# A rebuilt first stage, and g of tiles 4 to 7 moved, in a fused attention-and-MLP kernel scheduled by a list scheduler

## Chip, cores, metric

One core of one Trainium2 chip. The metric is the device time of one execution in microseconds. "Ratio" is always the mean time of one kernel's fast runs over the mean of the fast runs of the kernel before in the same rounds on the same chip, so it is not quite the ratio of the medians quoted beside it. The interval given with it is 95%.

## The reference

x is 2048 tokens by 448, bf16. After a layer norm it goes through linear attention with 16 heads of 28 (s) and through a squared-ReLU MLP of 1792 (whose silu is g). The output is x + s * g.

```python
def reference(A_x, A_wqkv, A_wo, B_x, B_w1, B_b1, B_w2, B_b2):
    # _A_ref: q, k, v = x @ wqkv; phi(t) = where(t > 0, t + 1, exp(t)) + 1e-6
    #   kv = sum_s phi(k) v, z = sum_s phi(k), o = phi(q) kv / (phi(q) z + 1e-6), o @ wo
    # _B_ref: relu(x @ w1 + b1)**2 @ w2 + b2
    x = A_x
    xn = _layernorm(x, axis=-1)
    s = _A_ref(xn, A_wqkv, A_wo)
    g = _silu(_B_ref(xn, B_w1, B_b1, B_w2, B_b2))
    return x + s * g
```

## The kernel before

The tokens are 16 tiles of 128, in four groups of four tiles. For each group the kernel computes K of each tile (phi of k), Q (three chunks), and H0 to H13 (the MLP's hidden layer, transposed). Then come the sums over tokens, the denominators, g of each tile, and S of each tile (attention output, multiplied by g). x is normalized, and must be transposed (xT) before any of these matmuls. The contraction is 448 = 3 x 128 + 64, so two units share the last 64 rows: their half-row matmuls run side by side on the two halves of TensorE ("pairs").

The program is a list of operations with modelled durations. A list scheduler decides, before anything runs, the order on each engine. TensorE and SyncE (SP) keep the order of the text; ACT, DVE and POOL take the ready operation that the model thinks is needed soonest. On the chip each engine then works through its fixed list and waits where it must.

```python
RATE = 262e3                    # modelled bytes per us of all loads together
LEAD = 8.0
# ... cut (in schedule): modelled transfers
                s2 = max(dma_free, st + 1.9)
                dma_free = s2 + op.nbytes / RATE
                op.end = dma_free + 0.7
# ... cut: loads, in issue order
        load_x(0, 1, "act")
        load_x(1, 2)                                   # on SP
        load_k("sp", w_qkv, A_wqkv, "wk", 384, 2 * D)  # K weights
        load_x(2, 4, "act")
        dma("act", b1r[:, :], B_b1.rearrange("(f p) -> f p", p=P), ["b1r"], F * 2).prio = -103
        load_w1("w1a", 0, 512)                         # h weights of H0 to H3
        load_x(4, 8)
        # ... cut: further weights; then the ACT table load, prio -101

        def pe_transpose(si, eng, prio):               # one tile: five transposes, one copy
            b = Buf("T")
            def f(e, _):
                v = ps(b)[:, :].bitcast(bf)
                for c in range(3):
                    e.transpose(v[:, c * P : (c + 1) * P], xn[:, si, c * P : (c + 1) * P], ident[:, :])
                e.transpose(v[0:64, 3 * P : 4 * P], xn[:, si, 384:448], ident[:, :])
                return e.transpose(v[64:P, 3 * P : 4 * P], xn[:, si, 384:448], ident[:, :])
            # ... cut: copy of the bank to xT on ACT or DVE

        def dma_transpose(si):                         # tiles 4 to 15 are transposed by a transfer
            op = add("sp", ...)                        # ... cut
            op.lead = LEAD + STAGGER * (3 - si % 4)    # how early it should be issued
# ... cut: the head
        warm(10, wide=True)                            # matmuls on zeros, to have the clock up
        pe_transpose(0, "act", -100)
        warm(2)
        pe_transpose(1, "dve", at_head["xT1"])
        pe_two(kk(0), kk(1), third_and_fourth)         # K0, K1; tiles 2 and 3 transposed between
        streams = (("H0 H1 H2 H3 K2 H4 K3 H6", "H5 Q0 Q1 H7 H8 H9 Q2 H11 H10 K0' H12 H13"), ...)
# ... cut: denominators. Their reciprocals go to DRAM and come back broadcast over partitions (rb);
#     DVE then multiplies q by them, group by group
        def replicate(eng, dst, src, h, step, n, name, reads):   # one broadcast; 19 in all
            # ... cut
            dma(eng, dst.rearrange("p (g t) -> p g t", g=NG), src, [name], dst.shape[0] * NG * n * 2, reads)
# ... cut: the last stage; (first g tile, first S tile of each pair)
        for i, *pairs in ((4, 0), (6, 2), (8, 4, 6), (10, 8), (12, 10, 12)):
```

Of the kernel before, what the change touches and what calls it, by code (L numbers as in the profile page):

```python
# [9 lines left out]
P = 128  # L10
# [7 lines left out]
RATE = 262e3  # L18
# [14 lines left out]
class Op:  # L33
    def __init__(self, eng, emit, reads, writes, dur, alts, nbytes):
        self.eng, self.emit, self.dur, self.alts, self.nbytes = eng, emit, dur, alts, nbytes
        self.reads, self.writes = list(reads), list(writes)
        self.raw, self.deps, self.succ = set(), set(), []
        self.start = self.end = None
        self.seq = None
        self.late = 1e9  # L40
        self.lead = LEAD
        self.prio = None
        self.sync = set()
# [10 lines left out]
class Program:  # L54
# [3 lines left out]
    ENGINES = ("pe", "act", "dve", "pool", "sp")  # L58
# [27 lines left out]
    def schedule(self):  # L86
# [25 lines left out]
        free["pool"] = free["dve"] = 0.8  # L112
# [7 lines left out]
        def ready(op):  # L120
            r = 0.0
            for d in op.deps:
                if d.end is None:
                    return None
                r = max(r, d.end + (0.0 if d.eng == op.eng == "pe" and d not in op.sync else LAT))
            return r
# [14 lines left out]
        while n:  # L141
# [69 lines left out]
            if op.nbytes:  # L211
                free[e] = st + op.dur
                s2 = max(dma_free, st + 1.9)
                dma_free = s2 + op.nbytes / RATE
                op.end = dma_free + 0.7
# [65 lines left out]
def bass_recurrent_scan__linear_attn_block__dense_activation_squared_relu__prompt_kernel(  # L281
    nc, A_x, A_wqkv, A_wo, B_x, B_w1, B_b1, B_w2, B_b2, out
):
    with ExitStack() as es:
# [5 lines left out]
        junk = sb("junk", [P, 512], bf)  # L290
# [14 lines left out]
        b1r = sb("b1r", [NF, P], bf)  # L305
# [33 lines left out]
        def pool(fn, writes, reads=(), dur=0.3):  # L339
            add("pool", fn, reads, writes, dur)  # L340
# [4 lines left out]
        add("dve", lambda e, _: e.memset(junk[:, :], 0.0), [], ["junk"], 0.2).prio = -1000  # L345
# [29 lines left out]
        pool(lambda e, _: e.memset(zmask[:, :, :], 1.0), ["zmask"])  # L375
# [19 lines left out]
        def load_x(lo, hi, eng="sp"):  # L395
            dma(eng, x_tok[:, lo:hi, :], x_r[:, lo:hi, :], [("x", i) for i in range(lo, hi)], (hi - lo) * P * D * 2)

        def load_k(eng, w, src, name, lo, hi, eng2=None):

            n = (hi - lo) * 2  # L400
            dma(
                eng, w[:, 0:3, lo:hi], src[0:384, lo:hi].rearrange("(c p) j -> p c j", p=P), [(name, 0)], 384 * n
            )
            for i in (0, 1):
                dma(eng2 or eng, w[64 * i : 64 * i + 64, 3, lo:hi], src[384:448, lo:hi], [(name, 1 + i)], 64 * n)

        def load_w1(name, lo, hi):


            dma(  # L410
                "sp", w_1[:, 0:3, lo:hi], B_w1[0:384, lo:hi].rearrange("(c p) j -> p c j", p=P), [(name, 0)],
                768 * (hi - lo),
            )
# [5 lines left out]
        wnames = lambda name: [(name, i) for i in range(3)]  # L419
        load_x(0, 1, "act")  # L420
        load_x(1, 2)
        load_k("sp", w_qkv, A_wqkv, "wk", 384, 2 * D)
        load_x(2, 4, "act")
        dma("act", b1r[:, :], B_b1.rearrange("(f p) -> f p", p=P), ["b1r"], F * 2).prio = -103
        load_w1("w1a", 0, 512)
# [4 lines left out]
        add("act", lambda e, _: e.preload_act_table_set("natural_log_exp_and_others"), [], ["actw"], 1.3).prio = -101  # L430

# [10 lines left out]
        def ln_stats(si, prio=(None, None)):  # L442
            add(
                "dve", lambda e, _: e.bn_stats(st6[:, si, :], x_tok[:, si, :]), [("x", si)], [("st", si)], 0.553  # L444
            ).prio = prio[0]
            add(
                "dve", lambda e, _: e.bn_aggr(mv[:, si, :], st6[:, si, :]), [("st", si)], [("mv", si)], 0.16
            ).prio = prio[1]

        def ln_rstd(lo, hi):  # L450
            c = slice(lo, hi)
            ts = range(lo, hi)
            add(
                "act",
                lambda e, _: e.activation(out=vep[:, c], in_=mv[:, c, 1], func=AF.Ln, bias=eps5[:, 0:1]),
                [("mv", i) for i in ts] + ["eps5", "actw"], [("vep", i) for i in ts], 0.2,
            )
            add(
                "act", lambda e, _: e.activation(out=rstd[:, c], in_=vep[:, c], func=AF.Exp, scale=-0.5),
                [("vep", i) for i in ts], [("rstd", i) for i in ts], 0.2,  # L460
            )

        def ln_norm(si, prio=None):
            add(
                "dve",
                lambda e, _: e.tensor_scalar(  # L466
                    out=xn[:, si, 0:D], in0=x_tok[:, si, :], scalar1=mv[:, si, 0:1],
                    scalar2=rstd[:, si : si + 1], op0=ALU.subtract, op1=ALU.mult,
                ),
                [("x", si), ("mv", si), ("rstd", si)], [("xn", si)], 0.43,  # L470
            ).prio = prio

        def ln_twin(lo, hi):

            ts = range(lo, hi)
            add(
                "dve", lambda e, _: e.tensor_copy(xn[:, lo:hi, 448:512], xn[:, lo:hi, 384:448]), [("xn", i) for i in ts],
                [("xd", i) for i in ts], 0.1 + 0.03 * (hi - lo),
            )

        def pe_transpose(si, eng, prio):
            b = Buf("T")

            def f(e, _):
                v = ps(b)[:, :].bitcast(bf)
                for c in range(3):
                    e.transpose(v[:, c * P : (c + 1) * P], xn[:, si, c * P : (c + 1) * P], ident[:, :])  # L487
                e.transpose(v[0:64, 3 * P : 4 * P], xn[:, si, 384:448], ident[:, :])  # L488
                return e.transpose(v[64:P, 3 * P : 4 * P], xn[:, si, 384:448], ident[:, :])

            add("pe", f, [("xn", si), "ident"], [b], 0.35)

            def ev(e, _):
                src = ps(b)[:, 0:256].bitcast(bf).rearrange("p (c k) -> p c k", c=4)
                dst = xT[:, :, si * P : (si + 1) * P]
# [4 lines left out]
            add(eng, ev, [b], [("xT", si)], 0.42 if eng == "dve" else 0.6).prio = prio  # L500

        def dma_transpose(si):
# [5 lines left out]
            op.lead = LEAD + STAGGER * (3 - si % 4)  # L508
# [43 lines left out]
        def pe_two(a, b, between):  # L552

            for u in (a, b):

                def f(e, _, u=u):
                    for k in range(3):
                        last = u.mm(e, 2, k, k == 0, False)
                    return last

                add("pe", f, u.reads, [u.bank], 3 * MM(u.n))
            between()

            def rest(e, _):
                a.mm(e, 0, 3, False, True)
                return b.mm(e, 1, 3, False, True)

            add("pe", rest, [r for u in (a, b) for r in [*u.reads, u.bank]], [a.bank, b.bank], MM(a.n) + 0.1)
            a.out()
            b.out()  # L570
# [20 lines left out]
        def kk(si):  # L591
# [10 lines left out]
            return Acc(b, [("xT", si)] + wnames("wk"), mm, lambda: phi(b, qk_of(si), ("pk", si), blocks), 512)  # L602
# [21 lines left out]
        def qq(g, m):  # L624
# [8 lines left out]
            reads = [("xT", 4 * g + i) for i in range(4)] + wnames("wq")  # L633
            return Acc(b, reads, mm, lambda: phi(b, pqT[:, m, g * 512 : (g + 1) * 512], ("pq", g, m), lambda a: a), 512)

        def hh(g, fi):
            b = Buf("H")

            def mm(e, h, c, start, stop):
                return e.matmul(  # L640
                    ps(b)[:, 0:512], w_1[half[h], c, fi * P : (fi + 1) * P], xT[half[h], c, g * 512 : (g + 1) * 512],
# [3 lines left out]
            def out():  # L645
# [9 lines left out]
                def sq(e, eng):  # L655
                    if eng == "dve":
# [5 lines left out]
            return Acc(b, [("xT", 4 * g + i) for i in range(4)] + wnames(w1_of(fi)), mm, out, 512)  # L662
# [333 lines left out]
        order = ["st0", "mv0", "st1", "mv1", "xn0", "st2", "xn1", "mv2", "st3", "mv3", "xT1", "xn2", "xn3", "xT2", "xT3"]  # L996
        at_head = {n: -100 + i for i, n in enumerate(order)}
        for si in range(4):
            ln_stats(si, (at_head[f"st{si}"], at_head[f"mv{si}"]))
            ln_rstd(si, si + 1)  # L1000
            ln_norm(si, at_head[f"xn{si}"])

        def warm(n, after=(), wide=False):
            b = Buf("W")

            def f(e, _):
                last = None
                for _i in range(n):
                    w = 512 if wide else P
# [3 lines left out]
            add("pe", f, ["junk", *after], [b], n * (0.426 if wide else 0.107))  # L1013
            return b

        warm(10, wide=True)
        pe_transpose(0, "act", -100)
        warm(2)
        pe_transpose(1, "dve", at_head["xT1"])

        def third_and_fourth():
            pe_transpose(2, "act", -100)
            pe_transpose(3, "dve", at_head["xT3"])

        pe_two(kk(0), kk(1), third_and_fourth)
        bb = Buf("B1")
        add(
            "pe", lambda e, _: e.transpose(ps(bb)[:, 0 : NF // 2].bitcast(bf), b1r[:, :], ident[0:NF, 0:NF]),
            ["b1r", "ident"], [bb], 0.1,
        )  # L1030
        add(
            "act", lambda e, _: e.activation(out=b1f[:, :], in_=ps(bb)[:, 0 : NF // 2].bitcast(bf), func=AF.Copy), [bb],
            ["b1f"], 0.25,
        )

        def quads(g, what):
# [11 lines left out]
            ("H0 H1 H2 H3 K2 H4 K3 H6", "H5 Q0 Q1 H7 H8 H9 Q2 H11 H10 K0' H12 H13"),  # L1048
# [4 lines left out]
        for g, (first, second) in enumerate(streams):  # L1053
            if g + 1 < NG:
                ln(4 * g + 4, 4 * g + 8)
            quads(g, first)
# [36 lines left out]
        for i, *pairs in ((4, 0), (6, 2), (8, 4, 6), (10, 8), (12, 10, 12)):  # L1093
            ga, gb = gg(i), gg(i + 1)
            us = [(ss(j), ss(j + 1)) for j in pairs]
            phase((ga, C), (gb, C))
            x, y = us[0]
            if len(us) == 1:
# [49 lines left out]
```

## Time and profile before

Median 143.47 us (three runs, 143.30 to 143.54). The profiled execution spans 142.0 us.

| what | us | where read |
|---|---|---|
| TensorE busy | 137.8 of 142.0 | busy table |
| copy of transposed tile 3 (xT3) ends | 9.56 | timeline |
| H0 to H3 | 9.62 to 12.65 | timeline |
| quad K2 H4 K3 H6 begins | 12.65 | matmul start times |
| from there to the last matmul start | 126.52 | matmul start times |

The busy table of the page (engine, busy us, share of the span, instructions):

```profile
PE 137.8 (97%) x1215; PEld 67.4 (47%) x1215; DVE 91.3 (64%) x218; ACT 78.7 (55%) x151; POOL 23.4 (17%) x37
```

The waits of TensorE (who waited for whom: total us, times, longest):

```profile
PE pb L1010 <- DVE junk L345: 1.3, 1, 1.3
PE pb L487 <- DVE xn L466: 0.2, 1, 0.2
```

Line 1010 is the warm-up and line 487 a transpose: both are over before 5.6 us. After that no wait is listed. A busy share alone does not say that TensorE works at its pace, so I also took each matmul's start from the trace and compared the step to the next one with columns / 2.4 ns. From 12.65 us to the end the steps that are visibly longer add up to 0.8 us, none by more than 0.11 us. So this part cannot be shortened by removing waits, and the head is where time can come from.

The chain of waits in the head (start us, us, what; followed back from the last instruction):

```profile
0.80 2.78 DMA x_tok<-in_A_x_dram
3.61 0.64 DVE st L444
...
6.35 0.34 PE pb L487 x3
...
6.87 1.43 PE pb L597 x6
...
9.14 0.44 DVE xT L497
...
9.62 3.19 PE pb L640 x28
12.81 0.86 PE pb L597 x8
```

It alternates between engines: load, stats on DVE (444), transposes (487), K0 and K1 (597), the copy of tile 3 on DVE (497), H0 to H3 (640), then the quad with K2. **H0 to H3 need all four tiles, so they wait for the last copy.** That copy in turn waits for TensorE, which has the transposes of tiles 2 and 3 behind K0 and K1: DVE ended the norm of tile 3 at 8.11 and then stood 1.0 us idle (last line below). Here is what DVE does from the first load to that copy (groups by shape; busy us, mean ns | idle us before):

```profile
L444 DVE BATCH_NORM_STATS2 st<-x_tok 128x6 f32<-128x448 bf16 x5 | 3.1, 610 | 2.4 <-DMA x_tok<-in_A_x_dram 2.4
L466 DVE TENSOR_SCALAR xn<-x_tok,mv,rstd 128x448 bf16<-128x448 bf16 x4 | 1.5, 382 | 0.0
L497 DVE COPY xT<-pb 128x512 bf16<-128x512 bf16 x2 | 0.8, 408 | 1.0 <-PE pb L489 1.0
```

Later in the run, around the first S, the timeline shows (start us, us, engine, line, operation, shapes, [idle before]): the add of g 3 (916), the casts of msb (776), and the multiplication of q by the broadcast reciprocals (866). S (971) follows without a wait.

```profile
95.22 0.62 DVE L916 TENSOR_TENSOR gbuf<-pb,b2b 128x448 bf16<-128x448 f32 x1 [1.76 <-PE pb L905]
...
95.98 1.19 DVE L776 CAST msb<-pb 128x448 bf16<-128x448 f32 x2
...
97.32 0.96 DVE L866 TENSOR_TENSOR pqT<-pqT,xT 128x1536 bf16<-128x1536 bf16 x1
...
99.11 0.35 PE L971 MATMUL pb<-msb,pqR 64*128 64x448 bf16 x2
```

### The profile page before, as it was taken

The page shows a single profiled execution, that of the slowest core. Times are in us where ns is not written, and L with a number is a line of the kernel's source. Part 1 is how long each engine was busy: PE and PEld are TensorE (multiplying, and loading weights), DVE is VectorE, ACT ScalarE, POOL GpSimd, SP SyncE. Part 2 cuts the span into 40 slices and gives each one's busy share as a digit, 9 for nine tenths or more (in the row PEclk, how much of TensorE's full clock was granted, in tenths as well). Part 3 has the DMA queues.
Part 4 walks back from the last instruction along what each step waited for, and adds up shares of the span by engine and source line. Part 5 has one row for each costly group of instructions (what it writes and reads, how often), then busy time and mean ns, then how long its engine had stood idle before and what let it go on. Part 6 is the DMA issues. An engine that isn't in the chain of part 4 may idle for free.

```text
span 142.0 us, 3024 instructions
## 1 busy us (share of the span) xinstructions
PE 137.8 (97%) x1215; PEld 67.4 (47%) x1215; DVE 91.3 (64%) x218; ACT 78.7 (55%) x151; POOL 23.4 (17%) x37
## 2 busy tenths in 40 slices
PE   6999999999999999999999999999999999999992
PEld 2344444444444444444445455654555555555482
DVE  0979698698897999678959900149852436052743
ACT  2667979889878898879799572323030211030220
POOL 6000000000000000000790000000050507350670
DMA  4997768999250300000000025891001110201022
GB/s 111 329 334 225 78 176 279 342 244 129 55 64 15 74 19 5 0 9 14 0 0 0 0 78 135 186 166 32 5 6 58 37 32 32 97 27 43 32 97 67
DMA packets 19809, 12.90 MB, mean 91 GB/s; under 512 B 9364, under 2 KB 19412, under 8 KB 19796
## 3 DMA queue, kind: packets, MB, share of 16 engines
q1 hardware_dynamic: 17644, 11.22, 32.5%
q10 hardware_dynamic: 2152, 1.50, 4.8%
q8 instruction: 9, 0.15, 0.4%
q14 instruction: 4, 0.03, 0.1%
HBM read 8.78 MB, written 2.10 MB: 77 GB/s over the span
## 4 chain that ended last, share of the span: by engine, by line
PE 93%; DVE 3%; DMA 2%; issue 0%; DVEq 0%
PE pb L905 30%; PE pb L640 30%; PE pb L597 8%; PE pb L971 8%; PE pb L672 6%; PE pb L628 6%; DMA x_tok<-in_A_x_dram 2%; DVE st L444 1%; PE pb L678 1%; PE pb L765 1%; PE pb L726 1%; PE pb L487 1%; PE pb L803 0%; DVE xn L466 0%; PE pb L488 0%; DVE xT L497 0%
## 5 line engine op out<-in xcount | busy, mean ns | idle before, releaser
L640 PE MATMUL pb<-xT,w 64*128 64x512 bf16 x392 | 50.8, 376 | 0.1
L905 PE MATMUL pb<-w,r 64*128 64x448 bf16 (+3 forms) x378 | 45.1, 343 | 0.0
L649 ACT ACTIVATE r<-pb,b1f 128x512 bf16<-128x512 f32 x56 | 34.9, 689 | 4.1 <-PE pb L640 4.1
L640 PEld LDWEIGHTS pb<-xT,w 64*128 64x128 bf16 x392 | 21.4, 94 | 23.3 <-ACT r L649 0.6
L905 PEld LDWEIGHTS pb<-w,r 64*128 64x128 bf16 (+1 forms) x378 | 22.9, 95 | 19.9 <-issue 1.2
L916 DVE TENSOR_TENSOR gbuf<-pb,b2b 128x448 bf16<-128x448 f32 (+1 forms) x16 | 9.3, 609 | 33.2 <-PE pb L905 33.2
L881 ACT ACTIVATE gbuf<-gbuf 128x448 bf16<-128x448 bf16 (+1 forms) x16 | 8.6, 565 | 36.2 <-DVE gbuf L916 34.4
L950 POOL TENSOR_TENSOR xn<-xn,x_tok 128x448 bf16<-128x448 bf16 x15 | 15.1, 1029 | 48.7 <-DVE xn L941 48.7
L597 PE MATMUL pb<-w_qkv,xT 64*128 64x512 bf16 (+1 forms) x106 | 17.6, 377 | 0.0
L628 PE MATMUL pb<-xT,w_qkv 64*128 64x512 bf16 x84 | 15.5, 376 | 0.0
L657 DVE TENSOR_TENSOR r<-r 128x512 bf16<-128x512 bf16 x38 | 13.2, 418 | 0.0
L382 POOL MEMSET kvm<- 128x2048 bf16 x1 | 1.8, 1804 | 65.0 <-DVE zb L622 65.0
L971 PE MATMUL pb<-msb,pqT 64*128 64x448 bf16 (+3 forms) x93 | 11.2, 343 | 0.0
L444 DVE BATCH_NORM_STATS2 st<-x_tok 128x6 f32<-128x448 bf16 x16 | 9.4, 612 | 2.4 <-DMA x_tok<-in_A_x_dram 2.4
L575 ACT ACTIVATE qk<-pb 128x512 bf16<-128x512 f32 x16 | 9.0, 594 | 3.3 <-PE pb L597 2.7
L585 DVE SCALAR_TENSOR_TENSOR qk<-pb,qk 128x512 bf16<-128x512 f32 x16 | 10.7, 686 | 0.2
L941 DVE TENSOR_TENSOR xn<-pb,gbuf 128x448 bf16<-128x448 f32 (+2 forms) x17 | 9.3, 590 | 1.9 <-ACT gbuf L881 1.5
L658 ACT ACTIVATE r<-r 128x512 bf16<-128x512 bf16 x18 | 10.4, 651 | 0.0
L597 PEld LDWEIGHTS pb<-w_qkv,xT 64*128 64x128 bf16 (+1 forms) x106 | 6.6, 94 | 6.5 <-DVE xT L497 0.3
L672 PE MATMUL pb<-qk,xn 128*128 128x448 bf16 x48 | 9.4, 353 | 0.0
L628 PEld LDWEIGHTS pb<-xT,w_qkv 64*128 64x128 bf16 x84 | 6.0, 94 | 5.0
L616 DVE TENSOR_TENSOR zacc<-zacc,qk 128x448 f32<-128x448 f32 x13 | 8.1, 622 | 0.3
(81 smaller groups left out, 98.6 us busy)
## 6 DMA issues: line engine op xcount, KB each, us to landing
out_dram<-xn SPq DMA_DIRECT2D x15, 112.0 KB, 1.7
w<-in_B_w_dram SPq DMA_DIRECT2D x1, 1568.0 KB, 9.7
x_tok<-in_A_x_dram SPq DMA_DIRECT2D x3, 448.0 KB, 4.4
w<-in_B_w_dram SPq DMA_DIRECT2D x2, 384.0 KB, 4.7
xT<-rows ACTq DMA_DIRECT2D x6, 112.0 KB
w<-in_B_w_dram SPq DMA_DIRECT2D x1, 576.0 KB, 5.3
xT<-rows SPq DMA_DIRECT2D x5, 112.0 KB
w_o<-in_A_wo_dram SPq DMA_DIRECT2D x1, 392.0 KB, 10.9
```

Source lines behind the costliest of these rows:

```text
L444: "dve", lambda e, _: e.bn_stats(st6[:, si, :], x_tok[:, si, :]), [("x", si)], [("st", si)], 0.553
L585: lambda e, _: e.scalar_tensor_tensor(out=slot, in0=src(), scalar=1.0 + 1e-6, in1=slot, op0=ALU.add, op1=ALU.max),
L597: return e.matmul(ps(b)[:, 0:512], xT[half[h], c, si * P : (si + 1) * P], w_qkv[half[h], c, 384 : 2 * D], start=start, stop=stop,)
L628: return e.matmul(ps(b)[:, 0:512], w_qkv[half[h], c, m * P : (m + 1) * P], xT[half[h], c, g * 512 : (g + 1) * 512], start=start, stop=stop,)
L640: return e.matmul(ps(b)[:, 0:512], w_1[half[h], c, fi * P : (fi + 1) * P], xT[half[h], c, g * 512 : (g + 1) * 512], start=start, stop=stop,)
L649: lambda e, _: e.activation(out=slot, in_=ps(b)[:, 0:512], func=AF.Relu, bias=b1f[:, fi : fi + 1]),
L657: return e.tensor_tensor(out=slot, in0=slot, in1=slot, op=ALU.mult)
L658: return e.activation(out=slot, in_=slot, func=AF.Square)
L672: last = e.matmul(ps(b)[:, 0:D], xn[:, si, c * P : (c + 1) * P], pk_of(si), start=(si == 0), stop=(si == NT - 1),)
L905: return e.matmul(ps(b)[:, 0:n], r2[half[h], fi, si * P : (si + 1) * P], w_2[half[h], fi, c], start=start, stop=stop)
L950: eng, lambda e, _: e.tensor_tensor(out=ob, in0=ob, in1=x_tok[:, si, c], op=ALU.add),
L971: return e.matmul(ps(b)[:, 0:n], q, m, start=start, stop=stop)
```

## The change

The intent is to have useful matmuls begin earlier and fill TensorE's gaps in the head. It has these parts:

1. x tile 0 on SP and tile 1 on ACT; the ACT table load ahead of ACT's issues; h weights of H0 to H3 in two parts.
2. Norm, transposes and copies of tiles 0 and 1 in column halves; only 128x128 transposes (the last 64 columns are copied beside themselves by DVE, so no half-row transposes).
3. H0 to H3 begin on the 256 tokens of tiles 0 and 1, and get the other 256 after tiles 2 and 3.
4. New modelled transfer times, a fixed order of DVE and ACT in the head, and less urgency for the transposes of tiles 4 to 7.
5. In the last stage, g 4 to 7 ahead of the first S.
6. Not in the cuts below: the warm-up matmuls read a constant instead of a tile that DVE must first fill, so they begin at 0.84 us instead of 1.26. No run takes this part back alone.

```diff
-RATE = 262e3
+RATE = 300e3
 ...
-                s2 = max(dma_free, st + 1.9)
+                s2 = max(dma_free, st + 1.75)
                 dma_free = s2 + op.nbytes / RATE
-                op.end = dma_free + 0.7
+                op.end = dma_free + 0.3
 ...
-        load_x(0, 1, "act")
-        load_x(1, 2)
+        table = add("act", lambda e, _: e.preload_act_table_set("natural_log_exp_and_others"), [], ["actw"], 0.1)
+        table.prio = -120
+        load_x(0, 1)
+        load_x(1, 2, "act").prio = -118
 ...
-        load_w1("w1a", 0, 512)
+        load_w1("w1a", 0, 512, 2)
 ...
-            op.lead = LEAD + STAGGER * (3 - si % 4)
+            op.lead = LEAD + STAGGER * (3 - si % 4) if si > 7 else 4.0 + 1.4 * (7 - si)
 ...
+        k0, k1 = kk(0), kk(1)
+        first = [hh(0, fi, 0) for fi in range(4)]
+        second = [hh(0, fi, 1, first[fi].bank) for fi in range(4)]
 ...
+        turn(0, 0, "act")
+        turn(0, 1, "act")
+        turn(1, 0, "act")
+        mains(k0, (0, 1), [("xT", 0, 0)] + wnames("wk")[:1])
+        turn(1, 1, "dve")
+        mains(k0, (2,), [("xT", 0, 1)])
+        k_mains(k1, 1)
 ...
+        h_mains(0)
+        h_mains(1)
+        head["xT2"] = pe_transpose(2, None, "act")
+        h_mains(2)
+        head["xT3"] = pe_transpose(3, None, "dve")
+        h_mains(3)
 ...
+        rests(k0, k1)
 ...
+        rests(first[0], first[2])
+        rests(first[1], first[3])
+        for eng, names in (
+            ("dve", "st0 mv0 st1 mv1 xn00 xn01 xd0 xn10 xn11 xd1 st2 mv2 xT11 st3 mv3 xn2 xd2 xn3 xd3 xT3"),
+            ("act", "ln0 ex0 ln1 ex1 xT00 xT01 xT10 ln2 ex2 b1 ln3 ex3 xT2"),
+        ):                                   # ... cut: each becomes the fixed order of its engine
+        pe_four(*second)
 ...
-        for i, *pairs in ((4, 0), (6, 2), (8, 4, 6), (10, 8), (12, 10, 12)):
+        phase((g4, C), (g5, C))
+        phase((g6, C), (g7, C))
+        phase((g5, C), (g4, C))
+        s0[0]()
+        phase((g7, C), (g6, C))
+        s0[1]()
+        for i, *pairs in ((8, 2, 4), (10, 6, 8), (12, 10, 12)):
```

## The prediction

> **What bounds it now.** TensorE: the busy table gives it 97% of a 142.0 us span. The timeline's matmul starts show more: from the K2/H4 quad, at 12.65 us, to the last S matmul at 139.4 us it streams at 1/2.4 ns per column; all excess over that adds up to 0.8 us (mostly 0.1 us steps where the row tiling changes). So time = start of the unbroken stream (12.65) + 126.8 us + tail (2.6 us). Only the head has idle time worth taking. The waits view shows no TensorE wait after 5.5 us, and S of tiles 0 and 1 starts unhindered at 99.1 us: moving g 4 to 7 ahead of it removes no wait. Worth 0.
>
> **The head now.** x tile 0 lands at 3.58 us, its norm ends at 5.45, five transposes follow (tiling changes of 93 and 124 ns around the 64-row pair; the Trainium skill, "TensorEngine Tiling (Array Packing)", Key Properties, says a mode change drains TensorE, and this trace agrees), ACT copy 6.08 to 6.68, K0 at 6.80, transposes 2 and 3 at 8.1 to 9.0, last DVE copy to 9.56, H0 to H3 as 28 half-row matmuls of 512 columns 9.62 to 12.65. K weights land at 5.77, first h weights at 7.32: loads don't hold it.
>
> **After, walked through with these durations (an estimate).** The table load goes first on ACT, but ACT's DMA issues overlap its activations (seen at 86.1 us), so x1 is not held back. Half norm ends near 5.15; transposes are 128x128 only, no tiling change; half copies on ACT take about 0.4 us; K0 starts about 6.0 instead of 6.8; K1 ends about 7.4. Then twelve 256-column matmuls (0.11 us each, 1.3 us) of H0 to H3 on tiles 0 and 1 fill the gaps around transposes 2 and 3. xT3 is ready about 9.6, as now (same DVE work). The rest of H0 to H3 is 0.4 us and 14 pairs of 256 columns, about 1.55 us. Weight loads should keep up: the fold's matmuls with 112-column weights take 51 ns each now. So K2/H4 begins about 11.4, not 12.65: gain 1.25 us. The floor is about 10.7.
>
> **What can be given back.** xT of tile 7 lands at 21.51 and is first used at 22.77: the slack equals the gain. The new order makes these transposes less urgent, and the K0/K1 phi sooner (their banks, free at 13.56 now, are needed by K3/H6). I expect 0.2 us of new wait in 10 to 24 us, possibly 0.6.
>
> **Time.** 143.47 - 1.25 + 0.2 = 142.4 us. Eight in ten: 141.7 to 143.2. Faster by over 2%: 0.04; within 2%: 0.94; slower by over 2%: 0.02.
>
> **What would show it.** First K0 matmul near 6.0; 128-row H matmuls of 256 columns at 7.4 to 9.5; K2/H4 begins 11.2 to 11.8; from there to the last matmul about 127 us; TensorE busy within 1 us of before; tail 2.6 us. Wrong if x1 lands after 4.5 us (table load held ACT's queue); the first h weights land after 8 us (two parts cost more issue time on SP); or TensorE waits for DVE copies or banks near 12, or xT at 21.
>
> **What would make it wrong.** A stall of half a microsecond or more at the second token group (nearly the same time); a slower clock ramp (warm-up matmuls run at 427 ns until 4.6 us); or head savings nearer the floor (141.5).

## The result, and the profile after

142.38 us median (six runs, 142.25 to 142.46) against 143.39 us (six runs, 143.25 to 143.54). The ratio is 0.9929 (0.9916 to 0.9942): 1.0 us faster. The profiled execution spans 141.2 us.

Busy table and TensorE's waits, as shown of before:

```profile
PE 137.8 (98%) x1225; PEld 68.4 (48%) x1225; DVE 92.0 (65%) x224; ACT 78.7 (56%) x152; POOL 22.9 (16%) x38
```

```profile
PE pb L1035 <- PEq L1203: 0.8, 1, 0.8
```

TensorE's busy sum is the same, 137.8 us; the work has only moved forward. The one wait listed is the start of the program. The head in the timeline (L614 is K, L661 is H, L474 is DVE's norm, L503 a transpose, L513 DVE's copy of a transposed tile):

```profile
6.16 0.85 PE L614 MATMUL pb<-w_qkv,xT 128*128 128x512 bf16 x2
...
7.87 0.82 PE L661 MATMUL pb<-xT,w 128*128 128x256 bf16 x6
...
8.79 0.40 DVE L474 TENSOR_SCALAR xn<-x_tok,mv,rstd 128x448 bf16<-128x448 bf16 x1
...
9.25 0.44 PE L503 MATMUL pb<-ident,xn 128*128 128x128 bf16 x4
...
9.53 0.49 PE L661 MATMUL pb<-xT,w 128*128 128x256 bf16 x3
9.73 0.42 DVE L513 COPY xT<-pb 128x512 bf16<-128x512 bf16 x1 [0.32 <-PE pb L503]
...
9.95 0.39 PE L614 MATMUL pb<-w_qkv,xT 64*128 64x512 bf16 x2
...
10.18 1.91 PE L661 MATMUL pb<-xT,w 64*128 64x256 bf16 x32
...
11.92 1.03 PE L614 MATMUL pb<-w_qkv,xT 64*128 64x512 bf16 x8
```

K0 begins at 6.16 instead of 6.80, the first H matmuls at 7.87 instead of 9.62, and the quad with K2 at 11.92 instead of 12.65. From the quad's start to the last matmul start it is 126.49 us, against 126.52 before. DVE's work up to the copy of tile 3, grouped as before:

```profile
L451 DVE BATCH_NORM_STATS2 st<-x_tok 128x6 f32<-128x448 bf16 x5 | 3.1, 615 | 3.4 <-DMA x_tok<-in_A_x_dram 3.4
...
L489 DVE COPY xn<-xn 128x64 bf16<-128x64 bf16 x4 | 0.7, 182 | 0.1
L474 DVE TENSOR_SCALAR xn<-x_tok,mv,rstd 128x256 bf16<-128x256 bf16 x2 | 0.7, 329 | 0.0
L474 DVE TENSOR_SCALAR xn<-x_tok,mv,rstd 128x192 bf16<-128x192 bf16 x2 | 0.7, 326 | 0.0
```

A half norm takes 329 or 326 ns where a whole one takes 382, so halving two tiles costs about 0.5 us of DVE; the four 64-column copies cost 0.7 us more. **The norm of tile 3 ends at 9.19 instead of 8.11, and its copy at 10.15 instead of 9.56.** And around the first S the order on DVE is another one: the multiplication of q (889) now comes first, and DVE stands 3.45 us waiting for the broadcast, with the add of g 3 (939) and the casts (799) behind it:

```profile
96.16 0.96 DVE L889 TENSOR_TENSOR pqT<-pqT,xT 128x1536 bf16<-128x1536 bf16 x1 [3.45 <-DMA xT<-rows]
...
97.23 0.62 DVE L939 TENSOR_TENSOR gbuf<-pb,b2b 128x448 bf16<-128x448 f32 x1
97.77 1.14 DVE L799 CAST msb<-pb 128x448 bf16<-128x448 f32 x2
```

### The profile page after: what moved, and what is told of

It is laid out like the page before. It is cut to its first block, busy times and chain, and to the rows that moved or that the text cites. A ratio compares the mean times of both kernels' runs of the same rounds, so it can differ in the third digit from the quotient of the medians.

```text
span 141.2 us, 3056 instructions
## 1 busy us (share of the span) xinstructions
PE 137.8 (98%) x1225; PEld 68.4 (48%) x1225; DVE 92.0 (65%) x224; ACT 78.7 (56%) x152; POOL 22.9 (16%) x38
## 4 chain that ended last, share of the span: by engine, by line
PE 98%; DVE 0%; issue 0%; DVEq 0%
PE pb L928 30%; PE pb L661 30%; PE pb L614 9%; PE pb L994 8%; PE pb L695 7%; PE pb L645 6%; PE pb L1035 3%; PE pb L503 1%; PE pb L701 1%; PE pb L788 1%; PE pb L749 1%; PE pb L826 0%; DVE xn L964 0%; PE pb L819 0%; DVE xn L973 0%; PE pb L784 0%
## 5 line engine op out<-in xcount | busy, mean ns | idle before, releaser
L661 PE MATMUL pb<-xT,w 64*128 64x512 bf16 (+2 forms) x408 | 51.3, 365 | 0.0
L661 PEld LDWEIGHTS pb<-xT,w 64*128 64x128 bf16 (+1 forms) x408 | 22.8, 94 | 22.1 <-ACT r L670 0.5
L614 PE MATMUL pb<-w_qkv,xT 64*128 64x512 bf16 (+1 forms) x106 | 17.9, 379 | 0.0
L679 ACT ACTIVATE r<-r 128x512 bf16<-128x512 bf16 x17 | 9.7, 651 | 0.0
L614 PEld LDWEIGHTS pb<-w_qkv,xT 64*128 64x128 bf16 (+1 forms) x106 | 6.7, 95 | 6.2 <-DVE xT L513 0.2
L592 ACT ACTIVATE pqT<-pb 128x512 bf16<-128x512 f32 x12 | 6.8, 597 | 3.1 <-PE pb L661 1.6
```

What stands on the lines that cost most here:

```text
L592: add("act", lambda e, _: e.activation(out=slot, in_=src(), func=AF.Exp), [buf, "actw"], [tile], 0.6)
L614: return e.matmul(ps(b)[:, 0:512], xT[half[h], c, si * P : (si + 1) * P], w_qkv[half[h], c, 384 : 2 * D], start=start, stop=stop,)
L661: return e.matmul(ps(b)[:, c0 : c0 + n], w_1[half[h], c, fi * P : (fi + 1) * P], xT[half[h], c, t : t + n], start=start, stop=stop,)
L679: return e.activation(out=slot, in_=slot, func=AF.Square)
```

## The experiments

Two theories of what holds the head: **A**, DVE's chain of norms and copies, which ends with the copy of tile 3; **B**, TensorE's own work from K0 on, and its clock, which in this profile came up only at about 6.7 us. And one question about the last stage: is the order of g and S really worth nothing? Twelve kernels ran, on three chips, four to a chip, with five rounds each. All gave correct results.

| run | copy of tile 3 ends | quad begins | difference | quad less first stats | quad to last matmul start | median us | ratio |
|---|---|---|---|---|---|---|---|
| before | 9.56 | 12.65 | 3.09 | 9.04 | 126.52 | 143.39 | 1 |
| after | 10.15 | 11.92 | 1.77 | 8.52 | 126.49 | 142.38 | 0.9929 |
| after_again | 9.92 | 11.69 | 1.77 | 8.38 | 126.49 | 142.33 | 0.9918 |
| no_two_tiles | 9.93 | 13.02 | 3.09 | 9.69 | 126.95 | 144.47 | 1.0065 |
| only_g_order | 9.85 | 12.94 | 3.09 | 9.31 | 126.52 | 143.50 | 0.9999 |
| whole_halves | 10.87 | 12.64 | 1.77 | 9.23 | 126.57 | 143.37 | 0.9998 |
| all_but_g_order | 10.16 | 11.94 | 1.77 | 8.52 | 127.17 | 143.22 | 0.9978 |
| loads_undone | 10.21 | 11.98 | 1.77 | 8.37 | 126.49 | 142.60 | 0.9952 |
| whole_halves2 | 10.10 | 11.87 | 1.77 | 8.57 | 126.49 | 142.51 | 0.9938 |
| xT11_act | 9.74 | 11.51 | 1.77 | 8.18 | 127.08 | 142.08 | 0.9907 |
| late_scale_old_g | 9.92 | 11.69 | 1.77 | 8.37 | 126.49 | 142.29 | 0.9909 |
| late_scale_xT11_act | 9.84 | 11.61 | 1.77 | 8.18 | 126.50 | 142.13 | 0.9895 |
| old_lead | 9.93 | 11.70 | 1.77 | 8.37 | 127.68 | 143.44 | 0.9976 |
| late_scale_xT11_twins | 10.05 | 11.82 | 1.77 | 8.46 | 126.49 | 142.19 | 0.9901 |

The table is read from start times in the traces. Its fourth column: the quad begins 1.77 us after the copy of tile 3 in every run that begins H0 to H3 on two tiles, and 3.09 us after it in every run that doesn't. Where H0 to H3 are one piece, they wait for that copy. Where they are two, nothing waits for it: in after it ends at 10.15, and the first matmul that reads it starts at 10.40, with no gap before it. The two are tied only by their common origin, the transposes of tile 3. These begin 0.06 us after DVE ends the norm of tile 3, and from there to the quad TensorE takes 2.68 us, in all eleven such profiles. Before them TensorE waited only 0.08 to 0.11 us. **So the norm of tile 3 on DVE sets the quad, and TensorE's own work is close behind it.**

The fifth column starts the count at DVE's first stats, which begin as x tile 0 lands (3.30 to 3.63 us, varying from run to run). It is 8.37 or 8.38 in the four runs whose head is that of the changed kernel (in loads_undone but for the loads) and had the clock up in time, although K0 began anywhere from 6.01 to 6.34; it is 8.52 in after and all_but_g_order, where the clock came late. This supports A, with the norm of tile 3 as the chain's end.

### after_again: the changed kernel once more

> The changed kernel, unchanged, to be the yardstick of its chip and to see how much the head varies from run to run. Ratio to before 0.993 (0.991 to 0.995). Theory A (the head is held by the DVE chain of norms and copies, which ends with the copy of transposed tile 3 at 10.15 us): first quad after H0 to H3 begins at 11.9 again, whatever the array's clock does. Theory B (the head is held by the half-rate clock, which lasted until 6.6 to 6.8 us in the first profile): if the clock comes up at another time in this profile, that quad moves with it, by up to 0.4 us.

Measured: 142.33 us (142.22 to 142.36), ratio 0.9918 (0.9905 to 0.9931). In this profile the clock was up for K0's first matmul at 6.17, where in the first one K0's first matmul still took 427 ns to the next. The norm and the copy of tile 3 ended 0.24 us earlier, and the quad began 0.24 us earlier. Of this, 0.09 us is x tile 0, which landed at 3.29 instead of 3.38. The other 0.15 us fit the clock's phase (as B says), but it acts through DVE's chain (as A says): the second half of tile 1 is transposed behind K0's two matmuls, and DVE copies it before it takes the stats of tile 3.

### no_two_tiles: H0 to H3 in one piece

```diff
-        first = [hh(0, fi, 0) for fi in range(4)]
-        second = [hh(0, fi, 1, first[fi].bank) for fi in range(4)]
+        second = [hh(0, fi) for fi in range(4)]
 ...
-        h_mains(0)
-        h_mains(1)
 ...
-        h_mains(2)
 ...
-        h_mains(3)
 ...
-        rests(first[0], first[2])
-        rests(first[1], first[3])
```

> The changed kernel, but H0 to H3 are computed in one piece of 512 columns after tiles 2 and 3, as before; all else stays. If beginning them on two tiles is the whole gain: TensorE idles between K1 (7.9) and the rests (10.0), H0 to H3 take 3.05 us from about 10.2, the next quad begins at about 13.2 us instead of 11.9, and the time is about 143.6, no better than before (ratio 1.00 to 1.005). If the earlier, halved first tiles were the gain instead, the next quad begins at about 12.4 and the ratio is about 0.996.

Measured: 144.47 us (144.02 to 144.60), ratio 1.0065 (1.0049 to 1.0080). The head went as expected (quad at 13.02). What I had not expected is 0.45 us more after it. The timeline shows it, with DVE's fixed order as the cause: the broadcast came late, the add of g 3 stood behind it, and g 6 could not have its bank.

```profile
97.97 0.96 DVE L889 TENSOR_TENSOR pqT<-pqT,xT 128x1536 bf16<-128x1536 bf16 x1 [4.18 <-DMA xT<-rows]
...
99.21 0.62 DVE L939 TENSOR_TENSOR gbuf<-pb,b2b 128x448 bf16<-128x448 f32 x1
...
99.89 2.44 PE L928 MATMUL pb<-w,r 64*128 64x448 bf16 x24 [0.28 <-DVE gbuf L939]
```

The profiled run (144.02) was the fastest of the six, the others took 144.45 to 144.60: about 0.45 us more, which no trace shows.

So part 3 carries the gain, and without it the rest of the change is slower than before.

### only_g_order: the kernel before, with only the new order of g and S

The edit is the last hunk of the change, alone.

> The kernel before with only the new order of g 4 to 7 and the S pairs. The S of tiles 0 and 1 had no wait before, so nothing is to be had: ratio 1.000 within 0.002. If the order had removed hidden waits, TensorE's excess over its streaming rate after 96 us would fall and the ratio would be 0.998 or less.

Measured: 143.50 us (143.23 to 143.68), ratio 0.9999 (0.9984 to 1.0013). On the kernel before, the order is worth nothing, as predicted.

### all_but_g_order: the changed kernel with the old order of g and S

The edit is the same hunk taken back.

> The changed kernel with the old order of g and S (S of tiles 0 and 1 after g 4 and 5). By the prediction the order is worth nothing, so the ratio stays 0.992 to 0.993. Rival: in the static order of the changed kernel DVE stands waiting for the broadcast of the denominators (3.4 us idle until 96.2 us) ahead of the add of g 3 and the casts of msb, which end at 98.9 us; the old order needs S of tile 0 at 98.4, so it waits 0.5 us or more, the ratio is 0.996 or above, and the new order is what keeps the head's gain.

Measured: 143.22 us (142.44 to 143.44), ratio 0.9978 (0.9955 to 1.0000): a wide spread, with two of six runs below 142.8, as a transfer that is late in some runs would give. The rival was right. In the profiled run (143.16 us) S of tile 0 stood waiting for the casts, which stood behind the broadcast:

```profile
96.22 0.96 DVE L889 TENSOR_TENSOR pqT<-pqT,xT 128x1536 bf16<-128x1536 bf16 x1 [3.50 <-DMA xT<-rows]
...
97.30 0.62 DVE L939 TENSOR_TENSOR gbuf<-pb,b2b 128x448 bf16<-128x448 f32 x1
97.83 1.14 DVE L799 CAST msb<-pb 128x448 bf16<-128x448 f32 x2
...
99.03 0.36 PE L994 MATMUL pb<-msb,pqR 64*128 64x448 bf16 x2 [0.51 <-DVE msb L799]
```

By start times the step into this S is 0.67 us longer than the streaming rate. **The same hunk that is worth nothing on the kernel before is worth about 0.8 us in the company of the rest** (143.22 against 142.33 to 142.38).

### late_scale_old_g: the old order, but the scheduler told that broadcasts land later

```diff
+        self.extra = 0.0
 ...
-                op.end = dma_free + 0.3
+                op.end = dma_free + 0.3 + op.extra
 ...
-                dma(eng, dst.rearrange("p (g t) -> p g t", g=NG), src, [name], ..., reads)
+                dma(eng, dst.rearrange("p (g t) -> p g t", g=NG), src, [name], ..., reads).extra = 3.0
```

This changes nothing that the kernel does. In the traces of this run and of all_but_g_order the order of operations differs on DVE alone: the first multiplication of q, and a short one that follows it, move behind the add of g 3 and the casts.

> The changed kernel with the old order of g and S, but its scheduler told that the broadcasts of the denominators land 3 us later, which puts the scaling of q of the first token group behind the add of g 3 and the casts of msb on DVE, as in the kernel before. If DVE standing in order at the broadcast, brought about by the change's new transfer constants, was what took 0.67 us from S of tile 0 (profile of the run with the old order), this returns to the changed kernel's time without the new order: ratio 0.9925 to 0.994, no TensorE wait at 98 to 99 us. If the old order of g itself was at fault, the ratio stays at 0.9975 or so.

Measured: 142.29 us (142.21 to 142.57), ratio 0.9909 (0.9884 to 0.9933), with the old order of g and S. DVE's order is again that of before, and S waits for nothing:

```profile
94.24 0.62 DVE L940 TENSOR_TENSOR gbuf<-pb,b2b 128x448 bf16<-128x448 f32 x1 [1.76 <-PE pb L929]
...
95.00 1.19 DVE L800 CAST msb<-pb 128x448 bf16<-128x448 f32 x2
...
96.88 0.96 DVE L890 TENSOR_TENSOR pqT<-pqT,xT 128x1536 bf16<-128x1536 bf16 x1 [0.69 <-DMA xT<-rows]
...
98.12 0.35 PE L995 MATMUL pb<-msb,pqR 64*128 64x448 bf16 x2
```

So the fault was DVE's order, and the new order of g and S is a way around it. That the change's own shorter modelled transfers brought it about was checked afterwards by running the schedulers alone, without the chip: all_but_g_order with the three old transfer constants gets DVE's old order here, and the kernel before with the three new ones gets the new order.

### whole_halves and whole_halves2: tiles 0 and 1 not halved

```diff
-            for j in (0, 1) if i < 2 else (None,):
+            for j in (None,):
 ...
-        turn(0, 0, "act")
-        turn(0, 1, "act")
-        turn(1, 0, "act")
+        turn(0, None, "act")
         mains(k0, (0, 1), [("xT", 0, 0)] + wnames("wk")[:1])
-        turn(1, 1, "dve")
+        turn(1, None, "dve")          # whole_halves2: this line ahead of mains(k0, ...)
```

(The names in the order lists and of the norm's tiles follow.)

> The changed kernel with the norm, transposes and copies of tiles 0 and 1 whole again (one DVE norm of 0.37 us instead of two of 0.28, one copy of 0.6 us instead of two of 0.4). K0 begins about 0.25 us later (6.4), but DVE has about 0.3 us less to do before tile 3. Theory A (DVE chain): the copy of tile 3 ends no later, 9.9 to 10.2, and the time changes by less than 0.15 us. Theory B (TensorE from K0 on): the next quad begins 0.2 to 0.3 us later, and the time rises by as much.

Measured: 143.37 us (143.08 to 143.80), ratio 0.9998 (0.9979 to 1.0016). Both theories missed: the whole gain was gone, with the copy of tile 3 at 10.87. But the experiment was at fault. It put the transposes of tile 1 behind K0 in TensorE's order, and K0 waited for the copy of tile 0 (0.69 us in the timeline), so tile 1, and all of DVE behind it, came late.

> The earlier run with whole first tiles lost the whole gain, but its TensorE order put the transposes of tile 1 behind K0, which waits for the copy of tile 0. Here both transposes come before K0, as in the kernel before. If that order was the fault, K0 begins at 6.6, K1 ends at about 8.0, the next quad begins 0.2 to 0.4 us later than with halves (11.9 to 12.3) and the ratio is about 0.995. If halving itself carries the gain, the ratio is again 0.999 to 1.000.

Measured: 142.51 us (142.40 to 142.57), ratio 0.9938 (0.9925 to 0.9950). K0 began at 6.50, the quad at 11.87. With a sound order, whole tiles lose 0.1 to 0.3 us against the halved ones. In the fifth column it is 0.2 (8.57 against 8.37 or 8.38). Halving is a small part of the gain.

### loads_undone: the loads of before

```diff
-        table.prio = -120
-        load_x(0, 1)
-        load_x(1, 2, "act").prio = -118
+        table.prio = -101
+        load_x(0, 1, "act").prio = -118
+        load_x(1, 2)
 ...
-        load_w1("w1a", 0, 512, 2)
+        load_w1("w1a", 0, 512)
```

> The changed kernel with the loads of before: x tile 0 on the ACT queue and tile 1 on SP, the table load after ACT's issues, the first h weights in one part. x tile 0 then lands about 0.2 us later (3.58 against 3.38 in the profiles of before and after), all of the head is tied to it, so the next quad after H0 to H3 begins 0.2 us later (about 11.9 to 12.1) and the time is 0.2 us longer, ratio 0.9935. If the parts of the h weights matter, the first 256-column matmul starts after 7.9 us and the loss is larger, 0.4 us or more.

Measured: 142.60 us (142.53 to 143.07), ratio 0.9952 (0.9936 to 0.9968): 0.2 us lost by the medians, up to 0.5 by the ratios (one run at 143.07 weighs in), at least what was expected from the landing of x tile 0 (3.58 against 3.38). The fifth column is that of after_again, 8.37 against 8.38: in this profile the head is late by the landing of x tile 0, and by nothing else. The first H matmul began at 7.84, as early as with the parts (7.87): cutting the h weights in two gained nothing by itself.

### old_lead: tiles 4 to 7 as urgent as before

```diff
-            op.lead = LEAD + STAGGER * (3 - si % 4) if si > 7 else 4.0 + 1.4 * (7 - si)
+            op.lead = LEAD + STAGGER * (3 - si % 4)
```

> The changed kernel with the old urgency of the transposes of tiles 4 to 7 (they land near 23.1 and 23.7 us and are first used at 24.0 and 24.9 in the changed kernel; 20.4 and 21.5, with use at 24.7 and 25.6, before). Theory: those transposes have slack either way, so they land about 2 us earlier and the time is the same unless the norms of tiles 4 and 5 now go ahead of the phi of K0 and K1 on DVE; then the quads after H0 to H3 wait for the two banks of K0 and K1 near 12 to 13 us, by 0.3 to 0.9 us, and the ratio is 0.995 to 0.999.

Measured: 143.44 us (142.66 to 144.00), ratio 0.9976 (0.9942 to 1.0010). TensorE lost 1.18 us in one step, at 13.74. The second branch of the expectation came true, with a somewhat other owner of the bank than I had named:

```profile
10.59 1.15 DVE L451 BATCH_NORM_STATS2 st<-x_tok 128x6 f32<-128x448 bf16 x2 [0.66 <-DMA x_tok<-in_A_x_dram]
...
12.00 0.30 ACT L461 ACTIVATE vep<-mv,eps 128x2 f32<-128x2 f32 x1 [0.76 <-DVE mv L452]
12.32 0.20 ACT L465 ACTIVATE rstd<-vep 128x2 f32<-128x2 f32 x1
12.44 2.41 ACT L670 ACTIVATE r<-pb,b1f 128x512 bf16<-128x512 f32 x4
...
13.74 1.04 PE L661 MATMUL pb<-xT,w 64*128 64x512 bf16 x8 [1.01 <-ACT r L670]
```

With more urgency, the norm of tiles 4 and 5 stands ahead of the relus of H0 to H3 on ACT. x of these tiles landed late, DVE waited for it, ACT waited for DVE, and H4 and H6 waited for the banks that the relus hold. In the changed kernel these relus start at 11.80. Part of this loss is the chance of the load: x of tiles 4 to 7 landed at 10.57 here, at 9.23 and 9.55 in the two profiles of the changed kernel, and two of the six runs took 142.66 and 142.69.

### xT11_act, late_scale_xT11_act, late_scale_xT11_twins: going further

```diff
-        turn(1, 1, "dve")
+        turn(1, 1, "act")
 ...
-            ("dve", "... st2 mv2 xT11 st3 ..."),
-            ("act", "... xT10 ln2 ..."),
+            ("dve", "... st2 mv2 st3 ..."),
+            ("act", "... xT10 xT11 ln2 ..."),
```

late_scale_xT11_act has this edit and that of late_scale_old_g (with the new order of g and S). late_scale_xT11_twins has in addition the 64-column copies of tiles 0 and 1 on POOL.

> The changed kernel with the copy of the second half of tile 1 on ACT instead of DVE (0.26 us off DVE's chain). Theory A (DVE chain to tile 3): the stats of tile 3 begin 0.15 us earlier, the copy of tile 3 ends near 9.75 instead of 9.92 to 10.15, and the next quad begins at about 11.5: 0.15 us faster than the changed kernel, ratio about 0.9915. Theory B (TensorE's own work and clock from 6.2 us on): the next quad stays at 11.7 to 11.9 and the ratio at 0.9925.

Measured: 142.08 us (141.93 to 142.63), ratio 0.9907 (0.9893 to 0.9921). Theory A's figures: copy of tile 3 at 9.74, quad at 11.51, and 0.2 us less in the fifth column (8.18). The profiled run was the slowest (142.63), and it lost 0.58 us to the late broadcast again:

```profile
96.70 0.96 DVE L889 TENSOR_TENSOR pqT<-pqT,xT 128x1536 bf16<-128x1536 bf16 x1 [4.41 <-DMA xT<-rows]
...
98.52 2.82 PE L928 MATMUL pb<-w,r 64*128 64x448 bf16 x28 [0.41 <-DVE gbuf L939]
```

> The changed kernel with the second half copy of tile 1 on ACT and the same later scaling, so that a late broadcast no longer holds the bank of g 3 (0.58 us lost in the profiled, slowest run of the earlier ACT variant; its other runs took 141.9 to 142.2). Next quad at about 11.5, no TensorE wait at 98 us, 142.0 us, ratio 0.9905, and no run above 142.4. If the late broadcast was not the cause of the slow run, one run in six again lies near 142.6.

Measured: 142.13 us, all six runs from 142.01 to 142.23, ratio 0.9895 (0.9869 to 0.9921). The quad came at 11.61, not 11.5, as x tile 0 landed later (3.40 against 3.31; 8.18 again in the fifth column), and no run was slow. This beats both kernels: 142.13 against 142.33 to 142.38 us of the changed one, though these ran in different sets of rounds. Six runs without a slow one agree with the cause but do not prove it.

> The same as the run with ACT's copy and the later scaling, and the 64-column copies of tiles 0 and 1 on POOL instead of DVE (0.18 us each off DVE). Theory A (DVE chain to tile 3 sets the head): tile 3's copy ends near 9.4 instead of 9.75, the next quad begins at 11.2 to 11.4, 0.15 to 0.3 us faster still, ratio about 0.989. Theory B (TensorE's own work from K0 on, or POOL's slower copy delaying the transposes): the next quad at 11.5 or later, no gain.

Measured: 142.19 us (142.09 to 142.36), ratio 0.9901 (0.9877 to 0.9926): no gain over the run without it on the same chip. In its profile the clock came up late (K0's first matmul ran at half rate), so its head is not to be compared closely. But DVE now waits for ACT, which copies the half tile before it takes the rstd of tile 2; freeing DVE further is of no use here while ACT keeps this order:

```profile
7.97 0.40 DVE L475 TENSOR_SCALAR xn<-x_tok,mv,rstd 128x448 bf16<-128x448 bf16 x1 [0.38 <-ACT rstd L466]
```

## Why the prediction was right

The total was right (142.4 against 142.38), and so was its mechanism. Two of its terms were off, and they cancelled in part.

- **Bound by the stream after the head: right.** 126.52 us before, 126.49 after, as long as nothing waits.
- **H0 to H3 on two tiles as the carrier: right.** From the copy of tile 3 to the quad it is 3.09 us in one piece and 1.77 us in two (predicted 1.8: 11.4 less 9.6); 1.53 us of the 1.77 read tile 3, and the copy is done 0.24 us before they begin. Undone, the gain is not only lost but reversed (1.0065).
- **"xT3 is ready about 9.6, as now (same DVE work)": wrong, the mis-sized term.** It ends at 9.92 (clock up in time) or 10.15 (clock late), where before had 9.56 and 9.85. Up to that copy DVE is busy 5.9 to 6.0 us (after_again, after) instead of 4.8 us. The words "same DVE work" leave out what the halves cost (the change's own model puts a half norm at 0.22 us, measured 0.33) and the four 64-column copies (0.18 us each), which the kernel before doesn't need for these tiles. So the norm of tile 3 ended at 8.95 to 9.19 (before: 8.11), and the quad began at 11.69 to 11.92 instead of 11.4. That DVE's chain to this norm sets the quad is shown by the fixed 0.06 and 2.68 us in eleven profiles, by the fifth column, and by the half copy moved to ACT (8.18 instead of 8.37). Less DVE work alone would not have given 11.4 (an estimate from the steps in these traces): TensorE waited only about 0.2 us for DVE between K0 and the quad (0.10 before the transposes of tile 3, 0.04 within those of tile 2 and of tile 3), K0 began at 6.16 and not 6.0, and in after the late clock took 0.26 us of K0's matmuls.
- **0.2 us given back at tiles 4 to 7: wrong, it was nothing.** I read that tile 7 is first used at 22.77 us before. The matmuls of that unit (K of tile 4) use tile 4; tiles 6 and 7 are first used at 24.76 and 25.63. Their real slack was about 4 us. The change spends 3 us of it (tile 7 lands at 23.74 and is used at 24.87), and gets for it the early relus and phi. That half of the sentence, that the new urgency serves the banks, was right. old_lead puts its worth at about 1 us by the medians and 0.7 to 0.8 us by the ratios, part of it the chance named there.
- **Moving g 4 to 7 "worth 0": right on the kernel before (0.9999), wrong in the changed kernel, where it saves about 0.8 us.** I judged it by waits in the profile before. But other parts of the same change, the shorter modelled transfers, moved the wait for the broadcast ahead of two operations on DVE; late_scale_old_g shows that this order alone makes the wait.
- **Loads: right that they hold nothing much** (0.2 to 0.5 us for all of part 1; x tile 0's earlier landing gives 0.2 to 0.3 of it). The table load did not hold ACT's issues: it runs from 0.80 to 2.08 and x tile 1 is issued at 0.83.

That the two wrong terms went against each other, a quad 0.3 to 0.5 us later than predicted and 0.2 us not given back, was luck, and it helped the total.

Left open: how much each of part 4's constants and its fixed order contribute, what the earlier warm-up (part 6) and the transposes without half rows (in part 2) are worth alone, and whether the 3 to 4.4 us by which broadcasts vary in DVE's idle time come from other transfers or from the broadcast itself.

## What to carry to other kernels

Where an engine works through a fixed order, ask of every wait what stands behind it in that order: a late transfer costs the time of whatever was queued behind the operation that needs it. A part of a change that does nothing alone may be what holds another part's gain, so test it both alone and by taking it out. A fixed distance between two events doesn't show that one sets the other: look whether the later one waited. And when an operation is halved, cost the halves by measured times of that size, not by columns: here two halves of a 0.38 us norm took 0.66 us.

## What the Trainium skill lacked or had wrong

- "TensorE: Matmul & The Clock Gate", Part 1, gives the half-rate and full-rate steps of a 512-column matmul as 426.7 and 215.7 ns, and the traces agree (427 and 216). It says the change of rate varies by 500 ns from run to run, and further down that its window is free-running and that one kernel can show 6, 11 or 14 slow matmuls; the traces fit the second statement better than the first. Here the warm-up began at 0.84 us in all runs with the changed head, and full rate came between 3.4 and 3.7 us in one run (late_scale_old_g) and at about 6.7 us in another (after): a spread of 3 us, worth about 0.15 us of time in after against after_again. The profile's clock column read 1.00 in the stretches of after that still ran at half rate; only the steps between matmul starts showed the half rate.
- "TensorEngine Tiling (Array Packing)", Key Properties, says that changing the tiling mode drains TensorE, without a figure. Here a change at full rate costs about 95 to 125 ns beyond the streaming step (93 and 124 around the half-row transposes of before, 96 at 9.95 us of after).
- "DMA: Bandwidth & Descriptors", Issuing engines are not separate DMA queues, says that issuing from several engines only saves issue time. The two load queues agree with it: x tiles 0 and 1 landed at 3.38 and 3.57 us whether 0 or 1 was on SP; the tile on SP was the earlier one by 0.2 us in all fourteen traces, which the page doesn't have.
- No page was found to say that a transfer issued by ACT goes out under a running table load (issued at 0.83 us, inside 0.80 to 2.08, and landed at 3.57).
